# GpSimd's last shift of a D tile written as a 32-bit integer addition

## The chip, the cores and the metric

The program runs on one core of one Trainium2 chip. The metric is the device time of one execution in microseconds (us). A core has five engines that run side by side and wait for each other by semaphores: PE (TensorE, matrix products), ACT (ScalarE), DVE (VectorE), POOL (GpSimd) and SP, which here only issues transfers.

## The reference

```python
def reference(A_x, A_wq, A_wk, A_wv, A_wo, B_x, B_w1, B_b1, B_w2, B_b2):
    def _A_ref(x, wq, wk, wv, wo):          # 2048 rows, 512 columns, 32 heads of 16
        q = (x @ wq).reshape(B, S, H, Dh).transpose(0, 2, 1, 3)
        k = x @ wk                          # one key and one value head for all
        v = x @ wv
        p = softmax(einsum("bhqd,bkd->bhqk", q, k) * (Dh ** -0.5))
        o = einsum("bhqk,bkd->bhqd", p, v)
        return o.transpose(0, 2, 1, 3).reshape(B, S, H * Dh) @ wo
    def _B_ref(x, w1, b1, w2, b2):          # 1792 hidden columns
        return gelu(x @ w1 + b1) @ w2 + b2
    x = A_x
    xn = layernorm(x)
    return x + _A_ref(xn, A_wq, A_wk, A_wv, A_wo) + _B_ref(xn, B_w1, B_b1, B_w2, B_b2)
```

Inputs and output are bf16. All but a small part of the time goes to the exponentials of the scores: 32 heads by 2048 by 2048.

## The kernel before

The prologue loads x in 16 tiles of 128 rows, normalizes them, transposes them on PE into `xnT`, and makes the keys `KT` (L829, ACT copies them out of PSUM), the values `V` and the first queries `QT`. Then comes the main loop. A score tile is 128 keys by 512 queries of one head; there are 2048 of them, taken in 683 units of three. For each unit PE makes the scores (L958) in one of two sets of three PSUM banks, so the scores of unit u+2 need every tile of unit u to have left its bank. A table in the source says which tiles go to which engine:

- ACT takes most of them: one exponential over two or three tiles (L981), written to `E`.
- DVE takes the others in another way. L1012 adds a constant to the scores and writes them as int16 to `Dt`; the bits of such a number, read as bf16, are a first approximation to the exponential (a "pattern"). Four more patterns come from it by adding small whole numbers to the 16-bit words. Two instructions on DVE make three of them in other buffers (L1059, over a batch of tiles); the last one, minus 26, is made in place, one instruction for each tile of 128x512 (L1055). Each pattern is multiplied with its own scaled copy of the values on PE (L1025), and the sum is the better approximation. The shift in place must wait until PE has read the unshifted pattern and DVE has made the others from it.

Between the units, PE also does the queries of later blocks, the two dense layers and the output projection (L672 and others), and DVE brings their results out of PSUM (L1071, L1139, L1167). L1102 on POOL normalizes the attention's output. L1336 are products with zeros that fill stretches in which PE would stand idle.

The order on every engine is fixed when the program is built. A planner (`Prog.schedule`) walks over all operations with costs of its own, and the engines then run that order. Three of its rules matter here. A shift in place (kind "pl") is put on POOL only beside a DVE instruction that is planned for 0.4 us or more and isn't itself a shift; the planned cost is `PL_OCC` = 0.62 us. If a shift has stood ready for 1.0 us, DVE takes it over (L1055 as DVE, planned at 0.2 us). And an operation of the prologue with a due time goes by that time only among those that are ready at the same moment: a free engine takes what there is. The prologue's operations on POOL are added by `setup`, and the due times of the rest (`DU`, `HP`, `QK`, `YP`) are numbers in the source. `add` records an operation with what it reads and writes, and the waits follow from that.

Of the kernel before, what the change touches and what calls it, by code (L numbers as in the profile page):

```python
# [7 lines left out]
ALU = mybir.AluOpType  # L8
AX = mybir.AxisListType

P = 128
# [7 lines left out]
SPL_STEPS = ((1, 0, 1, 26), (2, 0, 2, 51), (0, 0, 1, -26))  # L19
# [16 lines left out]
PL_OCC = 0.62  # L36
ON_OCC = 0.66
PL_LAT = 0.06
# [3 lines left out]
PL_DUE = 3.0  # L42
# [57 lines left out]
TBW = 512  # L100


def vcost(n, mode=1):
    return n / 0.96e3 / mode + 0.065
# [7 lines left out]
class Prog:  # L112
# [19 lines left out]
    def add(self, eng, fn, r=(), w=(), acc=None, dma=None, occ=0.1, lat=0.15, allow=1.0, kind=None, tag=None, after=(), due=None, lock=False, docc=0.0):  # L132
        op = _Op()
        op.lock, op.docc = lock, docc
        op.eng, op.fn = eng, fn
        op.stream = dma or eng
        op.amt = 16 if dma else 1
        op.need = bool(dma)
        op.ticket = None
        op.occ, op.lat, op.allow, op.kind, op.tag = occ, lat, allow, kind, tag  # L140
        op.idx = len(self.ops)
        op.done = False
        op.due = due
        op.rel = None
        op.pm = any(k == ("bank", 7) or k[0] == ("bank", 7) for k in w)
        deps, sdeps = {}, {}

        def dep(o, raw):
            if o is None or o is op:
                return  # L150
            if o.stream == eng == "pe":
                sdeps.setdefault(id(o), (o, False))
                return
            deps[id(o)] = o
            sdeps[id(o)] = (o, True)

        for k in r:
            dep(self.writer.get(k), True)
            for o in self.accs.get(k, ()):
                dep(o, True)  # L160
        for k in w:
            dep(self.writer.get(k), False)
            for o in self.readers.get(k, ()):
                dep(o, False)
            for o in self.accs.get(k, ()):
                dep(o, False)
        if acc is not None:
            dep(self.writer.get(acc), False)
            for o in self.readers.get(acc, ()):
                dep(o, False)  # L170
        op.deps = list(deps.values())
        for o in op.deps:
            o.need = True
        for k in w:
            self.writer[k] = op
            self.readers[k] = []
            self.accs[k] = []
        for k in r:
            self.readers.setdefault(k, []).append(op)
        if acc is not None:  # L180
            self.accs.setdefault(acc, []).append(op)
        for o in after:
            sdeps.setdefault(id(o), (o, True))
        if self.in_chain:
            o = self.chain.get(eng)
            if o is not None:
                sdeps.setdefault(id(o), (o, False))
            self.chain[eng] = op
        op.sdeps = list(sdeps.values())
        self.ops.append(op)  # L190
        return op
# [344 lines left out]
def bass_parallel_sum__grouped_kv_mqa__dense_activation_gelu__prompt_kernel(  # L536
# [15 lines left out]
    S, D = xf.shape  # L552
# [15 lines left out]
    i16, i32 = dt.int16, dt.int32  # L568

    with ExitStack() as es:  # L570
        def sb(shape, dtype, name):
            return es.enter_context(nc.sbuf_tensor(name, shape, dtype))
# [55 lines left out]
        mT = sb([32, TBW], bf, "mT")  # L628
        E = sb([P, NE, TBW], bf, "E")
        Dt = sb([P, ND + (SPL_NB - 1) * NR, TBW], i16, "Dt")  # L630
        Of = sb([P, 2, TBW], f32, "Of")
        den = sb([P, 2, 2, 16], f32, "den")
        OfP = sb([P, 2, TBW], f32, "OfP")
# [13 lines left out]
        add = pr.add  # L647

        def B(b):
            return ("bank", b)  # L650
# [32 lines left out]
        for i in range(8):  # L683
            e = X_Q[i]
            dma("sp" if e == "s" else "act", x_sb[:, 2 * i:2 * i + 2, :], x_view[:, 2 * i:2 * i + 2, :], f"d_x{i}",
                w=[("x", 2 * i), ("x", 2 * i + 1)], lat=X_LAT[i], due=0.0)
# [6 lines left out]
        def setup(fn, r=(), w=(), occ=0.16, due=0.0, lat=0.1, **kw):  # L693
            return add("pool", fn, r, w, occ=occ, lat=lat, due=due, **kw)
# [3 lines left out]
                                        pattern=[[-1, P]], channel_multiplier=1), r=["ident"], w=["ident"])  # L698
        setup(lambda e: e.memset(ones[:], 1.0), w=["ones"])
        zop = setup(lambda e: e.memset(zeros[:], 0.0), w=["zeros"])  # L700
        setup(lambda e: e.memset(mask4[:], 1.0), w=["mask4"])
        setup(lambda e: e.affine_select(out=mask4[:], in_=mask4[:], compare_op=ALU.is_ge, fill=0.0, base=0,
                                        pattern=[[-32, 4]], channel_multiplier=1), r=["mask4"], w=["mask4"])
# [8 lines left out]
              w=[(k, g, j) for k in ("QT", "QTm") for g in range(NGR) for j in range(HG)])  # L712
# [170 lines left out]
        for _, _, kind, a in sorted(steps, key=lambda s: s[:2]):  # L883
# [15 lines left out]
            due=0.0)  # L899
# [6 lines left out]
        for va, vb_ in ((0, NVA), (NVA, NT)):  # L906
            src = vsrc(va, vb_)
            dve(lambda e, src=src, va=va, vb_=vb_: e.tensor_copy(Vf[:, va:vb_, :], src), w=[vbank(va, vb_)[1], ("Vf", va)], n=(vb_ - va) * Dh,
                due=DU["vf"])
# [26 lines left out]
        def tile_of(t):  # L936
            gg, r = divmod(t, TPG)
            return gg, r // HG, r % HG
# [60 lines left out]
        dptr, size, base = [0, 0], [0], [0, 0]  # L999
# [24 lines left out]
        def pv_mm(gg, j, v, kt, rhs, r):  # L1024
# [2 lines left out]
                r=r + [("V", v, 0 if kt < NVA else NVA)], acc="O", occ=0.216, lat=dlat[1],  # L1027
                allow=4.0 if gg < NTB * NGR - 1 or kt < NT - 4 else -5.0, kind="pv", tag=(gg, j))

        def close_batch():  # L1030
            n = len(batch)
            have = {0: 0}

            def slot(b):
                return base[0] if b == 0 else ND + (b - 1) * NR + base[1]

            def view(b, nb):
                s = slot(b)
                step = (slot(b + 1) - s if nb > 1 else n) * TBW
                return bass.AP(Dt[:].tensor, Dt[:].offset + s * TBW, [list(Dt[:].ap[0]), [step, nb], [1, n * TBW]])  # L1040

            def sums(bufs):
                for b in bufs:
                    v = 1 + SPL_K.index(have[b])
                    for q, (t, _) in enumerate(batch):
                        gg, kt, j = tile_of(t)
                        pv_mm(gg, j, v, kt, Dt[:, slot(b) + q, :].bitcast(bf), [(("D", base[b > 0] + q), b)])

            for o, i, nb, k in SPL_STEPS:
                def keys(b):  # L1050
                    return [(("D", base[b + m > 0] + q), b + m) for m in range(nb) for q in range(n)]
                if o == i:
                    for q in range(n):
                        d = Dt[:, slot(o) + q, :]
                        add("pool", lambda e, d=d, k=k: e.tensor_scalar(d, d, 1.0, float(k), ALU.mult, ALU.add),  # L1055
                            [], [(("D", base[o > 0] + q), o)], occ=PL_OCC, lat=PL_LAT, allow=PL_DUE, kind="pl", lock=True,
                            docc=vcost(TBW, 4))
                else:
                    dve(lambda e, d=view(o, nb), q=view(i, nb), k=k: e.tensor_scalar(d, q, float(k), None, ALU.add),  # L1059
                        r=keys(i), w=keys(o), n=nb * n * TBW, mode=4, allow=1.0, kind="post", lock=True)  # L1060
                for m in range(nb):
                    have[o + m] = have[i + m] + k
                sums(range(o, o + nb))
            del batch[:]
# [257 lines left out]
        for i in (0, 1, 3, 2):  # L1322
            dst, key = ub[:, 6 + i, :], ("u", 0, 6 + i)
            w = [(B(FB[i]), j) for j in range(4)] + ([B(FB[i])] if i < 3 else []) + [key]
# [50 lines left out]
```

## Time and profile before

| | |
|---|---|
| time, median of 3 runs | 747.64 us (747.59 to 747.67) |
| the profiled execution's own time | 747.55 us |
| its span, first to last instruction | 745.8 us |
| busy on PE, DVE, ACT | 98% each |
| busy on POOL | 52% |
| shifts in place on POOL (L1055) | 459, 350.7 us busy |
| shifts in place on DVE (L1055) | 98, 25.7 us busy |
| granted TensorE clock | 1.0 all through |

A row of the groups reads: line, engine, operation, what is written and read, shapes, count, then busy time and the mean of one instruction, then the idle time of that engine just before them and who ended it. A row of the timeline begins with the start and the duration in us. Instructions of one engine overlap a little in these records: a DVE instruction that lasts 0.68 us is followed 0.60 us after its start by the next one. So the price of an instruction on a full engine is the distance from its start to the next start.

### The profile page before, as it was taken

The page shows a single profiled execution, that of the slowest core. Times are in us where ns is not written, and L with a number is a line of the kernel's source. Part 1 is how long each engine was busy: PE and PEld are TensorE (multiplying, and loading weights), DVE is VectorE, ACT ScalarE, POOL GpSimd, SP SyncE. Part 2 cuts the span into 40 slices and gives each one's busy share as a digit, 9 for nine tenths or more (in the row PEclk, how much of TensorE's full clock was granted, in tenths as well). Part 3 has the DMA queues.
Part 4 walks back from the last instruction along what each step waited for, and adds up shares of the span by engine and source line. Part 5 has one row for each costly group of instructions (what it writes and reads, how often), then busy time and mean ns, then how long its engine had stood idle before and what let it go on. Part 6 is the DMA issues. An engine that isn't in the chain of part 4 may idle for free.

```text
span 745.8 us, 22104 instructions
## 1 busy us (share of the span) xinstructions
PE 731.8 (98%) x9048; PEld 218.3 (29%) x9050; DVE 732.7 (98%) x1432; ACT 730.9 (98%) x743; POOL 391.4 (52%) x543
## 2 busy tenths in 40 slices
PE   7999999999999999999999999999999999999998
PEld 5322222222232222222232222322333222222223
DVE  8899999999999999999999999999999999999997
ACT  8899999999999999999999999999999999999995
POOL 5455555656433556555555455465564545646541
PEclk9999999999999999999999999999999999999999
DMA  9200100100010010100101010100100101010011
GB/s 312 66 9 24 32 8 18 24 10 16 16 46 22 18 39 17 25 16 16 27 10 28 25 38 17 37 18 12 23 16 19 34 18 38 16 40 23 11 31 36
DMA packets 32078, 23.34 MB, mean 31 GB/s; under 512 B 16369, under 2 KB 27498, under 8 KB 31978
## 3 DMA queue, kind: packets, MB, share of 16 engines
q1 hardware_dynamic: 30922, 21.90, 11.2%
q8 instruction: 72, 1.18, 0.7%
q14 instruction: 28, 0.23, 0.1%
q10 hardware_dynamic: 1056, 0.03, 0.1%
HBM read 13.08 MB, written 2.35 MB: 21 GB/s over the span
## 4 chain that ended last, share of the span: by engine, by line
ACT 61%; PE 30%; DVE 7%; issue 0%; DMA 0%; SPq 0%; POOL 0%
ACT E L981 60%; PE pAll L1025 13%; PE pAll L958 9%; PE pAll L672 7%; DVE Dt L1012 3%; DVE Dt L1059 2%; DMA x_sb<-in_A_x_dram 0%; DVE x_sb L1167 0%; ACT x_sb L1179 0%; PE pAll L810 0%; DVE stats L759 0%; ACT xnT L815 0%; PE pAll L666 0%; DVE Dt L1055 0%; DVE Of L1071 0%
## 5 line engine op out<-in xcount | busy, mean ns | idle before, releaser
L981 ACT ACTIVATE E<-pAll 128x1024 bf16<-128x1024 f32 (+1 forms) x677 | 680.0, 1263 | 1.9 <-PE pAll L958 1.8
L1055 POOL TENSOR_SCALAR Dt<-Dt 128x512 int16<-128x512 int16 x459 | 350.7, 764 | 303.1 <-DVE Dt L1059 128.4
L1025 PE MATMUL pAll<-Dt,V 128*32 128x512 bf16 x2785 | 406.2, 383 | 0.9 <-DVE Of L1071 0.5
L1012 DVE TENSOR_SCALAR Dt<-pAll 128x512 int16<-128x512 f32 (+1 forms) x545 | 368.6, 691 | 2.1 <-PE pAll L958 1.0
L1025 PE MATMUL pAll<-E,V 128*32 128x512 bf16 x1491 | 293.1, 383 | 0.0
L1059 DVE TENSOR_SCALAR Dt<-Dt 128x1024 int16<-128x1024 int16 (+5 forms) x560 | 292.3, 548 | 0.2
L958 PE MATMUL pAll<-QT,KT 32*128 32x512 bf16 x2048 | 267.1, 384 | 4.1 <-ACT E L981 0.9
L958 PEld LDWEIGHTS pAll<-QT,KT 32*128 32x128 bf16 x2048 | 66.7, 91 | 293.9 <-ACT E L981 283.1
L1025 PEld LDWEIGHTS pAll<-Dt,V 128*32 128x32 bf16 x2785 | 102.0, 95 | 101.5 <-issue 68.2
L672 PE MATMUL pAll<-xnT,w_sb 128*32 128x512 bf16 x896 | 85.0, 383 | 0.1
L1025 PEld LDWEIGHTS pAll<-E,V 128*32 128x32 bf16 x1491 | 69.4, 94 | 44.3 <-issue 32.2
L672 PE MATMUL pAll<-w_sb,x_sb 128*32 128x512 bf16 x448 | 68.0, 383 | 0.0
L672 PE MATMUL pAll<-w_sb,ub 128*32 128x512 bf16 x448 | 67.1, 383 | 0.2 <-DVE x_sb L1213 0.2
L672 PE MATMUL pAll<-wop,oTp 128*32 128x512 bf16 x256 | 56.8, 383 | 0.0
L1102 POOL TENSOR_TENSOR oTp<-OfP,rbP 128x256 bf16<-128x256 f32 x29 | 24.1, 837 | 27.2 <-DVE Dt L1055 14.6
L672 PEld LDWEIGHTS pAll<-xnT,w_sb 128*32 128x32 bf16 x896 | 22.1, 95 | 27.0 <-issue 16.3
L1055 DVE TENSOR_SCALAR Dt<-Dt 128x512 int16<-128x512 int16 x98 | 25.7, 281 | 0.0
L672 PE MATMUL pAll<-xnT,wq_sb 128*32 128x512 bf16 x256 | 23.2, 384 | 0.2 <-DVE ub L1167 0.2
L1071 DVE COPY Of<-pAll 128x512 f32<-128x512 f32 x31 | 21.1, 679 | 0.0
L1167 DVE TENSOR_SCALAR x_sb<-pAll,b1T 128x512 bf16<-128x512 f32 x28 | 20.7, 741 | 0.0
L1167 DVE TENSOR_SCALAR ub<-pAll,b1T 128x512 bf16<-128x512 f32 x28 | 20.7, 738 | 0.1
L672 PEld LDWEIGHTS pAll<-w_sb,x_sb 128*32 128x32 bf16 x448 | 16.8, 95 | 10.3 <-issue 7.9
(121 smaller groups left out, 261.9 us busy)
## 6 DMA issues: line engine op xcount, KB each, us to landing
OfP<-Of SPq DMA_DIRECT2D x124, 32.0 KB, 2.0
rbP<-rden_rows SPq DMA_DIRECT2D x124, 32.0 KB, 1.8
w_sb<-in_B_w_dram SPq DMA_DIRECT2D x2, 1792.0 KB, 12.8
x_sb<-in_A_x_dram SPq DMA_DIRECT2D x8, 256.0 KB, 4.3
x_sb<-in_A_x_dram SPq DMA_DIRECT2D x16, 128.0 KB, 2.2
QT<-qp SPq DMA_DIRECT2D x124, 16.0 KB, 1.8
out_dram<-x_sb SPq DMA_DIRECT2D x12, 128.0 KB, 1.9
wq_sb<-in_A_wq_dram SPq DMA_DIRECT2D x1, 512.0 KB, 6.2
```

The source lines that it names most:

```text
L672: add("pe", lambda e, c=c, j=j: e.matmul(o[c, :], l[:, c], rh, start=start, stop=stop, tile_position=(0, 32 * j)), r, [(k, j) for k in w] ...
L958: ins = e.matmul(o, l, rh, start=True, stop=True, tile_position=(q0, 0))
L981: o = act(lambda e: e.activation(E[:, s0:s0 + na, :], bank(b0, na).rearrange("p (a n) -> p a n", a=na), ACT.Exp, scale=LN2 / 128.0), w=[B( ...
L1012: op = dve(lambda e: e.tensor_scalar(Dt[:, s:s + n, :], bank(bk, n).rearrange("p (a n) -> p a n", a=n), float(127 * 128) + SPL_D, SPL_MIN, ...
L1025: add("pe", lambda e, a, b: e.matmul(pO[32 * j:32 * j + 32, :], V1[:, v, kt, :], rhs, start=a, stop=b, tile_position=(0, 32 * j)), r=r + [ ...
L1055: add("pool", lambda e, d=d, k=k: e.tensor_scalar(d, d, 1.0, float(k), ALU.mult, ALU.add), [], [(("D", base[o > 0] + q), o)], occ=PL_OCC, ...
L1059: dve(lambda e, d=view(o, nb), q=view(i, nb), k=k: e.tensor_scalar(d, q, float(k), None, ALU.add), r=keys(i), w=keys(o), n=nb * n * TBW, m ...
L1071: dve(lambda e: e.tensor_copy(Of[:, i, :], pO), w=["O", ("Of", i)], allow=0.0)
L1102: "pool", lambda e, c=c: e.tensor_tensor(oTp[0:n, sl, c], OfP[0:n, s, c], rbP[0:n, s, c], ALU.mult),
L1167: dve(lambda e: e.tensor_scalar(ubs[tb % 2][:, ft, :], pM, b1T[:, ft:ft + 1], None, ALU.add), r=["b1T"], w=M4 + [ukey(tb, ft)], n=TBW + 57 ...
```

## The change

The shift in place stays what it is for the values: minus 26 on each 16-bit pattern. On POOL it is now one integer addition on 32-bit words, each of which holds two patterns, so 256 words for a tile instead of 512 numbers. The second operand is one word, `k32`, read again and again (step 0). Its low half is -26 and its high half -27: the patterns are never under 64, so the low half always carries one into the high half, which makes -26 there too. `k32` is set by two more instructions on POOL. Where DVE takes a shift over, it runs the same instruction as before. The planned costs, the batches and the table of tiles are as they were.

```diff
+        k32 = sb([P, 2], i16, "k32")
...
         zop = setup(lambda e: e.memset(zeros[:], 0.0), w=["zeros"])
+        setup(lambda e: e.memset(k32[:, 0:1], SPL_STEPS[-1][3]), w=["k32"], due=24.0)
+        setup(lambda e: e.memset(k32[:, 1:2], SPL_STEPS[-1][3] - 1), w=["k32"], due=24.0)
         setup(lambda e: e.memset(mask4[:], 1.0), w=["mask4"])
...
+        def last_shift(e, d, k):
+            if e is not nc.gpsimd:
+                return e.tensor_scalar(d, d, 1.0, float(k), ALU.mult, ALU.add)
+            w = k32[:].bitcast(i32)
+            w = bass.AP(w.tensor, w.offset, [list(w.ap[0]), [0, TBW // 2]])
+            return e.tensor_tensor(d.bitcast(i32), d.bitcast(i32), w, ALU.add)
...
                         d = Dt[:, slot(o) + q, :]
-                        add("pool", lambda e, d=d, k=k: e.tensor_scalar(d, d, 1.0, float(k), ALU.mult, ALU.add),
-                            [], [(("D", base[o > 0] + q), o)], occ=PL_OCC, lat=PL_LAT, allow=PL_DUE, kind="pl", lock=True,
+                        add("pool", lambda e, d=d, k=k: last_shift(e, d, k),
+                            ["k32"], [(("D", base[o > 0] + q), o)], occ=PL_OCC, lat=PL_LAT, allow=PL_DUE, kind="pl", lock=True,
                             docc=vcost(TBW, 4))
```

The two new instructions also move others, since the planner takes a new course from the point where they stand. In the changed kernel the lines have other numbers: L702 and L703 set `k32`, the shift in place is L1038 on POOL and L1035 on DVE, L1012 is now L1015, L1059 is L1069, L829 is L832, L981 is L984.

On POOL in the prologue, about where the masks are made, the order was:

```order
L724 MEMSET crow 1x128
L728 MEMSET sel8 128x128
L729 MEMSET mask8 128x8
L725 MEMSET V1 128x96x16
L762 TENSOR_SCALAR nm<-sm 128x1
L730 AFFINE_SELECT mask8<-mask8 128x8
L727 MEMSET V1 128x16
L732 AFFINE_SELECT mask8<-mask8 128x8
```

It is now:

```order
L727 MEMSET crow 1x128
L731 MEMSET sel8 128x128
L732 MEMSET mask8 128x8
L702 MEMSET k32 128x1
L733 AFFINE_SELECT mask8<-mask8 128x8
L703 MEMSET k32 128x1
L735 AFFINE_SELECT mask8<-mask8 128x8
L728 MEMSET V1 128x96x16
L765 TENSOR_SCALAR nm<-sm 128x1
```

The two settings of `k32` have a due time of 24, yet stand where the masks are made, since POOL has a free moment there; the long setting of `V1` goes behind them.

On ACT at the prologue's end, where the keys (`KT`) are copied and the first exponentials (`E`) start, the order was:

```order
L815 ACTIVATE xnT<-pAll 128x4x256 x2
L829 ACTIVATE KT<-pAll,krow 128x512
L840 ACTIVATE oTp<-pAll 128x224
L844 ACTIVATE oTp,kmax<-pAll 128x16 x2
L829 ACTIVATE KT<-pAll,krow 128x512
L829 ACTIVATE KT<-pAll,krow 128x256
L981 ACTIVATE E<-pAll 128x1024
L829 ACTIVATE KT<-pAll,krow 128x512
L981 ACTIVATE E<-pAll 128x1024 x6
```

It is now:

```order
L818 ACTIVATE xnT<-pAll 128x4x256 x2
L843 ACTIVATE oTp<-pAll 128x224
L847 ACTIVATE oTp,kmax<-pAll 128x16 x2
L832 ACTIVATE KT<-pAll,krow 128x512 x2
L984 ACTIVATE E<-pAll 128x1024 x4
L832 ACTIVATE KT<-pAll,krow 128x256
L984 ACTIVATE E<-pAll 128x1536
L832 ACTIVATE KT<-pAll,krow 128x512
L984 ACTIVATE E<-pAll 128x1024 x6
```

One copy of keys moves from ahead of the squares (L840, now L843) to behind them, and one from ahead of the first exponential to behind the fourth.

The third place is the start of the main loop, POOL first. The order was:

```order
L921 TENSOR_SCALAR sel8R<-sel8,R2 128x128
L924 MEMSET wol 128x512
L925 CAST selL<-ident 128x4
L1055 TENSOR_SCALAR Dt<-Dt 128x512
L929 MEMSET b2row 128x512
L1055 TENSOR_SCALAR Dt<-Dt 128x512 x45
```

It is now:

```order
L924 TENSOR_SCALAR sel8R<-sel8,R2 128x128
L927 MEMSET wol 128x512
L928 CAST selL<-ident 128x4
L932 MEMSET b2row 128x512
L1038 TENSOR_TENSOR Dt<-Dt,k32 128x256 x33
```

And DVE in the same stretch, where it now has:

```order
L1069 TENSOR_SCALAR Dt<-Dt 128x512 x2
L1069 TENSOR_SCALAR Dt<-Dt 128x2x512 x2
L1015 TENSOR_SCALAR Dt<-pAll 128x512
L1035 TENSOR_SCALAR Dt<-Dt 128x512 x5
L1015 TENSOR_SCALAR Dt<-pAll 128x512
L1177 TENSOR_SCALAR ub<-pAll,b1T 128x512
```

Before POOL's first instruction on `oTp` there were 46 shifts in place on POOL, and there are 33. The thirteen others are on DVE: 111 of them in the whole program, where there were 98. All thirteen stand among the first 84 instructions of L1012. From there to the end the order is that of before on every engine: of DVE's instructions the last 1222 are the same in the same order, of PE's the last 7809, of ACT's the last 664. Up to there PE has 60 products with zeros of L1336 where it had 12, and in the prologue 29 of L1334 where it had 22; the other operations are the same ones, in another order.

## The prediction

> **What bounds the kernel now.** I read the page first, then the busy time by stretches, then the groups, then single rows of the timeline.
>
> ```profile
> PE 731.8 (98%) x9048; PEld 218.3 (29%) x9050; DVE 732.7 (98%) x1432; ACT 730.9 (98%) x743; POOL 391.4 (52%) x543
> ACT 61%; PE 30%; DVE 7%; issue 0%; DMA 0%; SPq 0%; POOL 0%
> core 0: us, PE busy (x) PEld busy (x) DVE busy (x) ACT busy (x) POOL busy (x), PEclk, DMA share, GB/s
> 30.00:106.00 76.00, 75.27 (x907) 21.82 (x909) 75.80 (x146) 76.00 (x75) 39.52 (x54) 1.00 0.08 20
> 106.00:725.00 619.00, 614.90 (x7678) 176.40 (x7670) 617.51 (x1183) 617.31 (x599) 329.72 (x427) 1.00 0.10 23
> L981 ACT ACTIVATE E<-pAll 128x1024 bf16<-128x1024 f32 x540 | 526.4, 1178 | 1.9 <-PE pAll L958 1.8
> L1055 POOL TENSOR_SCALAR Dt<-Dt 128x512 int16<-128x512 int16 x459 | 350.7, 764 | 303.1 <-DVE Dt L1059 128.4 <-PE pAll L1025 61.3 <-DVE Dt L1012 39.8
> L1012 DVE TENSOR_SCALAR Dt<-pAll 128x512 int16<-128x512 f32 x539 | 358.5, 679 | 2.1 <-PE pAll L958 1.0
> ```
>
> The chain ends on ACT for 61% of the span and on DVE for 7%, but that is a choice among equals: from 106 to 725 us ACT and DVE both stand idle for less than 2 us of 619. Each unit's scores wait for both, so a delay on either is paid nearly whole. POOL is idle for 303 us ahead of its shifts. Making POOL's instruction shorter therefore gains nothing by itself; what counts is what a POOL shift does to DVE.
>
> What it does shows where a POOL shift is still running when DVE begins a shift of its own (L1059). Three such meetings, each the shift on DVE and the POOL shift, the first one with the L1012 ahead of it:
>
> ```profile
> 93.23 0.68 DVE L1012 TENSOR_SCALAR Dt<-pAll 128x512 int16<-128x512 f32 x1
> 93.83 0.41 DVE L1059 TENSOR_SCALAR Dt<-Dt 128x1024 int16<-128x1024 int16 x1
> 93.27 0.62 POOL L1055 TENSOR_SCALAR Dt<-Dt 128x512 int16<-128x512 int16 x1
> ...
> 485.26 0.50 DVE L1059 TENSOR_SCALAR Dt<-Dt 128x1024 int16<-128x1024 int16 x1
> 484.86 0.62 POOL L1055 TENSOR_SCALAR Dt<-Dt 128x512 int16<-128x512 int16 x1
> ...
> 615.87 0.65 DVE L1059 TENSOR_SCALAR Dt<-Dt 128x1024 int16<-128x1024 int16 x1
> 615.61 0.62 POOL L1055 TENSOR_SCALAR Dt<-Dt 128x512 int16<-128x512 int16 x1 [2.50 <-PE pAll L1025]
> ```
>
> POOL ends 0.06, 0.22 and 0.36 us after DVE's shift has begun, and that shift lasts 0.41, 0.50 and 0.65: nothing, 0.09 and 0.24 us too long. So an overlap is free up to 0.13 us, and beyond that DVE waits for POOL's end. The planner lays each POOL shift (0.62) into one L1012 (0.60 from start to start), as in the first meeting. There is hardly any room behind it.
>
> **The change part by part.** Part A is the POOL instruction itself. No row shows a 32-bit integer addition; these are the nearest:
>
> ```profile
> L1055 POOL TENSOR_SCALAR Dt<-Dt x459: 620/622/2059, 28.0 to 732.8; 128x512 int16<-128x512 int16 x153
> L1102 POOL TENSOR_TENSOR oTp<-OfP,rbP x29: 719/783/1374, 94.4 to 718.5; 128x256 bf16<-128x256 f32 x29
> L782 POOL TENSOR_TENSOR nmr<-nm,rstd x4: 192/278/367, 5.4 to 16.6; 128x1 f32<-128x1 f32 x3, 128x2 f32<-128x2 f32 x1
> L875 POOL COPY oTp<-wq_sb 128x256 bf16<-128x256 bf16 x1 | 0.4, 393 | 0.0
> L914 POOL TENSOR_SCALAR V<-oTp 128x256 bf16<-128x256 f32 x5 | 4.3, 865 | 5.5 <-DVE oTp L908 5.1
> ```
>
> Now: 512 numbers, one input, 0.62 undisturbed. New: 256 words, two inputs of 4 bytes, the second one a repeated word. L1102 has that form (256 numbers, two inputs of 4 bytes): its shortest took 0.719, and 14 of its 29 lie between that and 0.740. Against the 0.192 of one number (L782) this is (0.719 - 0.192) / 255 = 2.07 ns a number, where the shift in place takes (0.620 - 0.192) / 511 = 0.84 ns. Half as many elements at 2.5 times the price is no gain. I take 0.727, the middle of those fourteen: 0.107 longer than now. The bounds are 0.393 (256 numbers with one input, L875) and 0.865 (256 numbers in pieces of 16, L914).
>
> The Trainium skill says the same against the change ("GPSIMD Engine Reference", section 3.1): a two-input instruction on GpSimd costs about 2.6 cycles an element, because both operands come through one read port. As an estimate from that page, 256 x 2.6 / 1.2 GHz is 0.55 us, and 0.19 for the start makes 0.75; the sum would then be 755.0 instead of 753.7.
>
> What a longer shift costs I counted on the trace. For each of the 459 POOL shifts I took its end and the start of the next shift on DVE; what a lengthening pushes beyond the free 0.13 us is paid. Today 20 of them are over, for 1.7 us. At +0.06 it is 1.4 us more, at +0.107 54 are over and it is 3.6 us more, at +0.15 6.2, at +0.20 14.0 (208 over), at +0.245 23.7. It is a cliff, since the slots were laid out for 0.62. At 0.393 almost all of today's 1.7 us goes: -1.6. Forecast for A: +3.6. Nothing of it is hidden, by the stretches above.
>
> PE waits for POOL's result only rarely:
>
> ```profile
> PEld pAll L958 <- ACT E L981: 283.1, 658, 0.9
> PEld pAll L1025 <- POOL Dt L1055: 2.7, 12, 0.2
> ```
>
> Twelve waits of at most 0.2 would become longer by 0.1, some 1.3 us in all, and that hides in the 283 us that PE waits for ACT's banks; if that cover were gone, 1.3 us is the price. Taken at nothing.
>
> Part B is the thirteen shifts that go from POOL to DVE at the start of the main loop. Such a shift is followed after 0.20 us:
>
> ```profile
> 315.25 0.28 DVE L1055 TENSOR_SCALAR Dt<-Dt 128x512 int16<-128x512 int16 x1
> 315.45 0.42 DVE L1059 TENSOR_SCALAR Dt<-Dt 128x1024 int16<-128x1024 int16 x1
> 24.40 0.69 DVE L1012 TENSOR_SCALAR Dt<-pAll 128x512 int16<-128x512 f32 x1 [0.43 <-PE pAll L958]
> 27.00 0.69 DVE L1012 TENSOR_SCALAR Dt<-pAll 128x512 int16<-128x512 f32 x1 [0.35 <-PE pAll L958]
> ```
>
> 13 x 0.20 = 2.6 us. Hidden would be what falls into DVE's two waits at the start, 0.43 + 0.35 = 0.8; from 30 to 106 us it is busy for 75.80 of 76.00 and hides nothing. The twelve additional groups of four products with zeros on PE (48) cost 0.21 each if PE had no gap for them, 2.5 in all:
>
> ```profile
> 301.32 0.40 PE L1336 MATMUL pAll<-xnT,zeros 128*32 128x512 bf16 x4
> 302.24 0.61 PE L1336 MATMUL pAll<-xnT,zeros 128*32 128x512 bf16 x8
> ```
>
> They lie in PE's wait for ACT, and I take nothing for them. Bounds for B: 1.8 to 5.1; taken 2.6, since most of the thirteen stand in the full stretch.
>
> Part C is the prologue. Two settings of 0.10 us stand ahead of the long one of `V1` on POOL, whose users come later; POOL has 0.5 us free right behind:
>
> ```profile
> L715 POOL MEMSET epsc<- 128x1 f32 x1 | 0.1, 102 | 0.0
> 8.74 0.30 POOL L777 TENSOR_SCALAR nm<-mv 128x2 f32<-128x2 f32 x1 [0.51 <-DVE mv L773]
> 20.10 0.58 ACT KT L829
> 21.85 0.69 ACT L829 ACTIVATE KT<-pAll,krow 128x512 bf16<-128x512 f32 x1 [0.45 <-PE pAll L666]
> 23.38 0.47 ACT L829 ACTIVATE KT<-pAll,krow 128x256 bf16<-128x256 f32 x1 [0.84 <-PE pAll L666]
> 24.39 1.02 ACT L981 ACTIVATE E<-pAll 128x1024 bf16<-128x1024 f32 x1 [0.54 <-PE pAll L958]
> ```
>
> The wait for `k32` is over long before the first shift at 28 us. The new order is another matter. It takes the copy of keys at 20.10 off the chain that ends last (0.58 gained), and it puts the smaller copy behind four exponentials (0.47 more on a full ACT). I set these against each other: 0, between -0.6 and +0.5.
>
> Sum: the profiled execution took 747.55 (span 745.8), 0.09 below the median of 747.64. 747.55 + 3.6 + 2.6 + 0 = 753.75, say 753.7. By the same bounds, A of 1.4 to 7.2 (+0.06 to +0.16) and B with C of 1.2 to 4, the forecast's own range is 750.2 to 758.7.
>
> **The rivals.** *The addition is quick.* If integers go through like a copy, 0.393 for 256 words, DVE never waits: 747.55 - 1.6 + 2.6 = 748.5. For it speaks that whole words need no conversion; against it that the second input must be read too, and L1102 pays for that. The Trainium skill ("GPSIMD Engine Reference", section 4.1) calls such an addition native, and section 3.1 has short loops at about one cycle an element; no row of this case shows it.
>
> *The addition is slow.* From about +0.16 the slots of the planner no longer hold. At 0.865 as in L914: 747.55 + 23.7 + 2.6 = 773.9. For it speaks that the integer path may be less polished than the usual one; against it that L914 reads and writes in short pieces, which this one doesn't.
>
> *The new start is quicker, and the kernel faster.* Between 21 and 25 us ACT waits for 0.45 + 0.84 + 0.54 = 1.8 us. In the new order both large copies of keys stand there in a row. If ACT sets the pace in the first units, those 1.8 us are work brought forward and the thirteen shifts run beside it. With a quick addition: 747.55 - 1.8 - 1.6 = 744.2; with A as forecast 749.4. It decides for faster when the addition takes less than about 0.63. Against it: behind 30 us DVE is as full as ACT.
>
> **How the numbers follow.** Forecast 0.55, quick addition 0.17, slow 0.18, quicker start 0.10. 0.2% is 1.5 us, about what a measurement of this kernel can tell from no change. Slower: the forecast (0.55), the slow case (0.18), and a quarter of the quick one with B above its middle (0.04): 0.77. Within: most of the quick one (0.11) and part of the last (0.04): 0.15. Faster: 0.06 + 0.02 = 0.08. The range: 748 leaves out the faster part and some of the quick case (about 0.1), 765 the upper half of the slow case (0.09).
>
> **What would show it.** Right: POOL's shifts 446, shortest between 0.71 and 0.75; L1059 on DVE with a larger mean in the same shapes, by some 4 us in sum from 106 us on, with the same orders there; DVE's L1055 111 times; from 0 to 106 us some 2.6 us more. Wrong: a shortest POOL shift near 0.4 (then the gain is at most 1.6) or above 0.8 (then the cliff); a first exponential well before 24.4 us; a DVE that waits for PE by the amount that the collisions cost, so that it was ACT's pace all along.

## The result, and the profile after

| | before | changed |
|---|---|---|
| time, median | 747.62 us (747.58 to 747.67, 4 runs) | 753.62 us (753.60 to 753.70, 4 runs) |
| span of the profiled execution | 745.8 us | 751.9 us |

The ratio is 1.0080 (95% interval 1.0068 to 1.0093): 6.0 us slower, and within 0.1 us of the forecast. The runs below show that this agreement is an accident: the forecast's largest term is zero, and what cost the time isn't in its sum.

The page of the changed kernel, busy times and four groups (L961 makes the scores, as L958 did before; a row reads line, engine, operation, written and read, count, then busy us and mean ns, then idle time ahead of them and who ended it):

```profile
PE 736.3 (98%) x9105; PEld 218.4 (29%) x9105; DVE 735.7 (98%) x1445; ACT 732.0 (97%) x743; POOL 371.7 (49%) x532
L984 ACT ACTIVATE E<-pAll 128x1024 bf16<-128x1024 f32 (+1 forms) x677 | 681.2, 1255 | 5.5 <-PE pAll L961 5.2
L1038 POOL TENSOR_TENSOR Dt<-Dt,k 128x256 int32<-128x256 int32 x446 | 331.3, 755 | 326.7 <-DVE Dt L1069 149.4
L1015 DVE TENSOR_SCALAR Dt<-pAll 128x512 int16<-128x512 f32 (+1 forms) x545 | 370.2, 694 | 4.8 <-PE pAll L961 3.3
L1069 DVE TENSOR_SCALAR Dt<-Dt 128x1024 int16<-128x1024 int16 (+5 forms) x560 | 292.3, 549 | 0.2
```

The durations of the integer addition (shortest, median, longest in ns), from the view of one line:

```profile
L1038 POOL TENSOR_TENSOR Dt<-Dt,k x446: 605/613/2051, 43.4 to 738.9; 128x256 int32<-128x256 int32 x149
```

Two stretches of the changed kernel, the same two as the prediction shows of before:

```profile
30.00:106.00 76.00, 74.97 (x893) 21.79 (x891) 73.05 (x148) 73.23 (x73) 25.54 (x37) 1.00 0.09 20
106.00:725.00 619.00, 614.87 (x7685) 175.44 (x7682) 617.46 (x1183) 617.31 (x600) 322.65 (x431) 1.00 0.10 23
```

Three things are to be seen. The addition takes 0.605 us at its shortest and 0.613 at the median, a little *less* than the old shift (0.620 and 0.622). L1069, DVE's own shifts, add up to 292.3 us, and it was 292.3 before: they are not longer by 4 us. And from 106 us on DVE and ACT are as busy as before (617.51 and 617.31 there). What is new lies ahead of 106 us: ACT is idle for 76.00 - 73.23 = 2.8 us of a stretch where it had no gap, and L984 waits 5.2 us for PE in the whole program where L981 waited 1.8.

The start of an exponential, compared with the start of the one with the same number in the kernel before, tells where the delay grows. The first is 0.32 us late, the third 0.75, the seventh 3.28, the thirteenth 4.21, the twenty-first 5.11, the thirty-third (64 us) 6.11; the hundredth is 6.07 late, and so is the last. So 0.32 us come from the prologue (in six later runs with the prologue of before the first exponential starts between 0.20 earlier and 0.04 later) and 5.75 from the first forty units of the loop.

The wait view of ACT between 24 and 106 us says for whom (total us, times, longest):

```profile
ACT E L984 <- PE pAll L961: 3.9, 8, 0.6
```

And the timeline of ACT shows when. First the start, in single rows:

```profile
24.71 1.02 ACT L984 ACTIVATE E<-pAll 128x1024 bf16<-128x1024 f32 x1
26.23 1.02 ACT L984 ACTIVATE E<-pAll 128x1024 bf16<-128x1024 f32 x1 [0.49 <-PE pAll L961]
27.74 1.02 ACT L984 ACTIVATE E<-pAll 128x1024 bf16<-128x1024 f32 x1 [0.49 <-PE pAll L961]
29.26 1.02 ACT L984 ACTIVATE E<-pAll 128x1024 bf16<-128x1024 f32 x1 [0.49 <-PE pAll L961]
30.18 0.47 ACT L832 ACTIVATE KT<-pAll,krow 128x256 bf16<-128x256 f32 x1
30.88 1.45 ACT L984 ACTIVATE E<-pAll 128x1536 bf16<-128x1536 f32 x1 [0.23 <-PE pAll L961]
32.38 0.69 ACT L832 ACTIVATE KT<-pAll,krow 128x512 bf16<-128x512 f32 x1
```

PE's score products in the same stretch, and the loads of weights (PEld) that stand in front of them:

```profile
25.79 0.39 PE L961 MATMUL pAll<-QT,KT 32*128 32x512 bf16 x3 [0.54 <-DVE Dt L1069]
27.31 0.39 PE L961 MATMUL pAll<-QT,KT 32*128 32x512 bf16 x3
25.79 0.10 PEld L961 LDWEIGHTS pAll<-QT,KT 32*128 32x128 bf16 x3 [0.81 <-ACT E L984]
27.30 0.10 PEld L961 LDWEIGHTS pAll<-QT,KT 32*128 32x128 bf16 x3 [0.43 <-ACT E L984]
```

And the remaining four of ACT's eight waits, from its grouped timeline:

```profile
39.20 1.45 ACT L984 ACTIVATE E<-pAll 128x1536 bf16<-128x1536 f32 x1 [0.60 <-PE pAll L961]
41.25 7.55 ACT L984 ACTIVATE E<-pAll 128x1024 bf16<-128x1024 f32 x7 [0.60 <-PE pAll L961]
49.34 11.66 ACT L984 ACTIVATE E<-pAll 128x1024 bf16<-128x1024 f32 x11 [0.54 <-PE pAll L961]
61.50 9.41 ACT L984 ACTIVATE E<-pAll 128x1024 bf16<-128x1024 f32 x9 [0.49 <-PE pAll L961]
```

ACT and PE take turns here. An exponential starts at 24.71 and ends at 25.73. PE begins the next scores at 25.79, when it is over, and the next exponential starts 0.44 us after that, at 26.23. (The first row of the products puts PE's idle time down to a shift on DVE; the loads of weights for the same products name ACT's exponential.) One turn takes 1.52 us, where two such exponentials in a row take 0.92 (shown with the ninth run). That is what happens when two units in a row use the same set of banks: PE has no second set to fill while ACT empties the first.

The planned order of the exponentials, by units (even units use one set, odd units the other), with the pairs that follow each other on one set:

```
before:  0 2 1 4 3 6 5 8 7 10 9 12 11 14 13 16 15 ...
changed: 0 2 4 6 8 10 1 12 3 14 5 7 9 16 11 18 13 20 15 17 22 19 24 21 26 23 28 25 30 27 29 32 31 ...
pairs, before:  0-2
pairs, changed: 0-2 2-4 4-6 6-8 8-10   5-7 7-9   15-17   27-29
```

The nine pairs of the changed order are the nine places in question: 26.23, 27.74, 29.26, 30.88, 32.97 (there a copy of keys fills the gap), 39.20, 41.25, 49.34 and 61.50. Why six even units come first can be read from the source: the keys' products go through bank 4, which belongs to the odd set, so no odd unit can start ahead of the last of them, and its copy now stands behind the fifth exponential. The odd units then had to catch up, and each one that caught up made another pair. The pair 0-2 stands in both orders; before, a copy of keys lies between its exponentials. So eight pairs are new.

The size fits as well, roughly. The eight steps with a wait (from one exponential's start to the next one's) are 5.0 us longer than such a step without one, the steps right behind them 0.8 in sum, and one more copy of keys stands behind the first exponential (30.18, 0.4 us on a full ACT). Less the 0.3 us by which the order of before falls short of an even pace, that is 5.9, against 5.75 measured.

### The profile page after: what moved, and what is told of

Its sections match the earlier page's. It is cut to its first block, busy times and chain, and to the rows that moved or that the text cites. A ratio compares the mean times of both kernels' runs of the same rounds, so it can differ in the third digit from the quotient of the medians.

```text
span 751.9 us, 22222 instructions
## 1 busy us (share of the span) xinstructions
PE 736.3 (98%) x9105; PEld 218.4 (29%) x9105; DVE 735.7 (98%) x1445; ACT 732.0 (97%) x743; POOL 371.7 (49%) x532
## 4 chain that ended last, share of the span: by engine, by line
ACT 60%; PE 29%; DVE 10%; issue 1%; DMA 0%; SPq 0%
ACT E L984 58%; PE pAll L1028 12%; PE pAll L961 9%; PE pAll L673 6%; DVE Dt L1015 4%; DVE Dt L1069 3%; PE pAll L1346 1%; DMA x_sb<-in_A_x_dram 0%; PE pAll L667 0%; DVE Dt L1035 0%; DVE x_sb L1177 0%; ACT x_sb L1189 0%; DVE stats L762 0%; ACT xnT L818 0%; DVE ub L1177 0%
## 5 line engine op out<-in xcount | busy, mean ns | idle before, releaser
L984 ACT ACTIVATE E<-pAll 128x1024 bf16<-128x1024 f32 (+1 forms) x677 | 681.2, 1255 | 5.5 <-PE pAll L961 5.2
L1038 POOL TENSOR_TENSOR Dt<-Dt,k 128x256 int32<-128x256 int32 x446 | 331.3, 755 | 326.7 <-DVE Dt L1069 149.4
L1015 DVE TENSOR_SCALAR Dt<-pAll 128x512 int16<-128x512 f32 (+1 forms) x545 | 370.2, 694 | 4.8 <-PE pAll L961 3.3
L1069 DVE TENSOR_SCALAR Dt<-Dt 128x1024 int16<-128x1024 int16 (+5 forms) x560 | 292.3, 549 | 0.2
L961 PE MATMUL pAll<-QT,KT 32*128 32x512 bf16 x2048 | 267.1, 384 | 4.5 <-ACT E L984 0.7
L961 PEld LDWEIGHTS pAll<-QT,KT 32*128 32x128 bf16 x2048 | 66.6, 90 | 294.8 <-ACT E L984 282.9
L673 PE MATMUL pAll<-xnT,w_sb 128*32 128x512 bf16 x896 | 84.0, 383 | 0.4 <-DVE ub L1177 0.2
L673 PE MATMUL pAll<-w_sb,x_sb 128*32 128x512 bf16 x448 | 68.0, 383 | 0.0
L673 PE MATMUL pAll<-w_sb,ub 128*32 128x512 bf16 x448 | 67.1, 383 | 0.2 <-DVE x_sb L1223 0.2
L673 PE MATMUL pAll<-wop,oTp 128*32 128x512 bf16 x256 | 56.8, 383 | 0.0
L673 PEld LDWEIGHTS pAll<-xnT,w_sb 128*32 128x32 bf16 x896 | 21.7, 95 | 28.0 <-issue 16.5
L1035 DVE TENSOR_SCALAR Dt<-Dt 128x512 int16<-128x512 int16 x111 | 28.9, 283 | 0.0
L673 PE MATMUL pAll<-xnT,wq_sb 128*32 128x512 bf16 x256 | 24.0, 384 | 0.0
L673 PEld LDWEIGHTS pAll<-w_sb,x_sb 128*32 128x32 bf16 x448 | 16.8, 95 | 10.3 <-issue 7.9
```

What stands on the lines that cost most here:

```text
L673: add("pe", lambda e, c=c, j=j: e.matmul(o[c, :], l[:, c], rh, start=start, stop=stop, tile_position=(0, 32 * j)), r, [(k, j) for k in w] ...
L961: ins = e.matmul(o, l, rh, start=True, stop=True, tile_position=(q0, 0))
L984: o = act(lambda e: e.activation(E[:, s0:s0 + na, :], bank(b0, na).rearrange("p (a n) -> p a n", a=na), ACT.Exp, scale=LN2 / 128.0), w=[B( ...
L1015: op = dve(lambda e: e.tensor_scalar(Dt[:, s:s + n, :], bank(bk, n).rearrange("p (a n) -> p a n", a=n), float(127 * 128) + SPL_D, SPL_MIN, ...
L1035: return e.tensor_scalar(d, d, 1.0, float(k), ALU.mult, ALU.add)
L1038: return e.tensor_tensor(d.bitcast(i32), d.bitcast(i32), w, ALU.add)
```

## The experiments

The theories at the start: the *longer instruction* (part A of the prediction), the *thirteen shifts* on DVE (part B), and a third, that the *order* costs by something else. Each time was taken in five rounds beside the kernel before, on the same chip.

**One: the integer addition in the order of before.** The two settings of `k32` are put into the operation that sets `epsc`, so that the planner has the same operations as before and makes the same order.

```diff
-        setup(lambda e: e.memset(k32[:, 0:1], SPL_STEPS[-1][3]), w=["k32"], due=24.0)
-        setup(lambda e: e.memset(k32[:, 1:2], SPL_STEPS[-1][3] - 1), w=["k32"], due=24.0)
...
-        setup(lambda e: e.memset(epsc[:], 1e-5), w=["epsc"], due=2.0)
+        def set_k32_epsc(e):
+            e.memset(k32[:, 0:1], SPL_STEPS[-1][3])
+            e.memset(k32[:, 1:2], SPL_STEPS[-1][3] - 1)
+            return e.memset(epsc[:], 1e-5)
+
+        setup(set_k32_epsc, w=["epsc", "k32"], due=2.0)
```

> The integer addition on POOL in the order of before: k32 is set together with epsc, as one step of the planner, so that PE, DVE, ACT and SP run exactly the order of before. The recorded sum (a POOL shift 0.107 longer) expects 751.2. The theory that the whole loss lies in the order expects 747.6, within 0.3, since the shortest POOL shift is 0.605 in the trace of the change against 0.620 before.

Measured: 747.45 us, ratio 0.9999 (0.9991 to 1.0008). The addition, by the view of its line:

```profile
L1041 POOL TENSOR_TENSOR Dt<-Dt,k x459: 603/612/2052, 27.8 to 732.7; 128x256 int32<-128x256 int32 x153
```

All 459 additions are there, and the time is that of before. Part A is zero.

**Two: the old shift in the new order.**

```diff
-            if e is not nc.gpsimd:
+            if True:
                 return e.tensor_scalar(d, d, 1.0, float(k), ALU.mult, ALU.add)
```

> The changed kernel's order on every engine, k32 set but not used: the shifts on POOL are the tensor_scalar instruction of before. The recorded sum expects 750.1 (only the thirteen shifts on DVE). The theory of the order expects 753.6, within 0.3.

Measured: 753.69 us, ratio 1.0081 (1.0068 to 1.0095). The whole loss is in the order, whatever instruction POOL runs.

**Three: `k32` set late.** The two settings wait until the prologue's other settings on POOL are through.

```diff
-        setup(lambda e: e.memset(k32[:, 0:1], SPL_STEPS[-1][3]), w=["k32"], due=24.0)
-        setup(lambda e: e.memset(k32[:, 1:2], SPL_STEPS[-1][3] - 1), w=["k32"], due=24.0)
...
+        setup(lambda e: e.memset(k32[:, 0:1], SPL_STEPS[-1][3]), w=["k32"], due=24.0, after=late)
+        setup(lambda e: e.memset(k32[:, 1:2], SPL_STEPS[-1][3] - 1), w=["k32"], due=24.0, after=late)
```

> The change with k32 held back until the first query mask is there (like wol and b2row), so that the planner gives PE, DVE, ACT and SP the order of before and only two short settings more stand on POOL. The recorded sum expects 751.2, the theory of the order 747.6, within 0.4.

Measured: 747.5 us, ratio 0.9999 (0.9990 to 1.0008). Two instructions of 0.1 us cost 6 us in one place of the plan and nothing in another.

**Four: the changed order, its fourteen early shifts back on POOL.** (Fourteen went to DVE and one came back; the fourteen are meant.)

```diff
         pr.schedule()
+        shifts = sorted((o for o in pr.ops if o.kind != "fill" and o.docc), key=lambda o: o.idx)
+        for n in (0, 2, 3, 4, 5, 6, 12, 16, 18, 19, 20, 23, 29, 42):
+            assert shifts[n].eng == "dve"
+            shifts[n].eng = shifts[n].stream = "pool"
```

> The changed kernel's order, but the fourteen early shifts that went from POOL to DVE are back on POOL, at the same place of the sequence. If thirteen shifts on DVE cost 0.20 each, 751.0 (2.6 less than 753.6). If the units in the wrong order set the time of this stretch alone and DVE has room there, 753.6. If these shifts stand behind POOL's later ones and are waited for, more than 753.6.

Measured: 755.32 us, ratio 1.0104 (1.0089 to 1.0120), 1.7 us more than the changed kernel. In this order the shifts are better off on DVE, so they can't be what costs 2.6 us there. Three of ACT's waits behind 45 us, by its timeline:

```profile
48.04 1.45 ACT L984 ACTIVATE E<-pAll 128x1536 bf16<-128x1536 f32 x1 [0.33 <-PE pAll L961]
50.21 11.60 ACT L984 ACTIVATE E<-pAll 128x1024 bf16<-128x1024 f32 x11 [0.72 <-PE pAll L961]
73.10 3.88 ACT L984 ACTIVATE E<-pAll 128x1024 bf16<-128x1024 f32 x3 [0.48 <-PE pAll L961]
```

Two more waits, of 0.33 and of 0.48, and the one that was 0.54 is 0.72. That the shifts come late on POOL and what needs them with them would explain this; it wasn't tried apart.

**Five: the order of before, the same fourteen shifts on DVE.** The edit is that of run four, made in the kernel before, with "dve" and "pool" in each other's place.

> The kernel before, unchanged but for fourteen early shifts in place, which run on DVE at the same place of the order. Theory 'thirteen shifts cost 0.20 us each' (the prediction's part B): DVE is full there, so 14 x 0.20 = 2.8 us, 750.4. Theory 'the order of the first score units costs the 6 us': this order is that of before, so whatever the shifts cost is no part of the 6 us; after the run with the shifts back on POOL (755.3 against 753.6) it expects less than 2.8, 747.6 to 749.

Measured: 749.89 us, ratio 1.0030 (1.0019 to 1.0042). This lies above the 749 that the theory of the order allowed, and close to the 750.4 of the theory of the shifts. The exponentials fall back from 35 us on, by 1.86 us at the forty-first and 2.2 at 106 us. The stretches:

```profile
30.00:106.00 76.00, 74.39 (x877) 21.30 (x879) 75.95 (x155) 74.93 (x74) 30.31 (x40) 1.00 0.09 20
106.00:725.00 619.00, 614.90 (x7684) 176.65 (x7677) 617.55 (x1184) 617.30 (x599) 327.41 (x428) 1.00 0.09 23
```

DVE is busy for 75.95 of 76.00 and ACT has 1.1 us of gaps. So the price of part B was nearly right for the order of before, 2.3 of 2.8 us; it is wrong for the order in which the shifts really stand, where DVE has gaps (73.05 of 76.00 in the changed kernel).

**Six and seven: new prologue with the old loop, old prologue with the new loop.** The planned list of operations is cut at the first score unit (behind 331 operations of before, 334 of the changed kernel) and put together crosswise. Run six sets `k32` as run one does. This is its edit; that of run seven is made in the same way.

```diff
         pr.schedule()
+        START = [14, 24, 0, 1, 9, 2, 16, 15, 25, 17, 47, 3, 18, 21, 19, 22, -1, 20, 4, -1, 23, 28,
...
+        pr.ops = new + pr.ops[331:]
```

> Integer addition on POOL; the prologue in the changed kernel's order up to the first score unit (but with every key copy where it was before), the main loop in the order of before, shifts on the engines of before. Theory 'order of the first score units': only the 0.32 us by which the first exponential starts later remain, 747.9. Theory 'the prologue's new order costs it': nearly all of the 6 us, 753 or more.

> The counterpart: the prologue in the order of before (the keys of tiles 10 and 11 copied ahead of the first exponential), and behind it everything in the changed kernel's order: the last keys' copy behind the sixth exponential, six even units ahead of the first odd one, the shifts on DVE. Theory 'order of the first score units': 753.6 less 0.32 = 753.3. Theory 'the prologue's new order costs it': 748 or less.

Measured: the new prologue with the old loop 749.20 us, ratio 1.0022 (1.0013 to 1.0031); the old prologue with the new loop 754.26 us, ratio 1.0088 (1.0074 to 1.0101). The first one's start on ACT:

```profile
25.52 0.47 ACT L835 ACTIVATE KT<-pAll,krow 128x256 bf16<-128x256 f32 x1 [0.70 <-PE pAll L667]
25.89 1.02 ACT L987 ACTIVATE E<-pAll 128x1024 bf16<-128x1024 f32 x1
27.12 0.69 ACT L835 ACTIVATE KT<-pAll,krow 128x512 bf16<-128x512 f32 x1 [0.21 <-PE pAll L667]
27.71 2.84 ACT L987 ACTIVATE E<-pAll 128x1024 bf16<-128x1024 f32 x3
```

And the second one's:

```profile
25.89 1.02 ACT L984 ACTIVATE E<-pAll 128x1024 bf16<-128x1024 f32 x1 [0.58 <-PE pAll L961]
28.69 1.02 ACT L984 ACTIVATE E<-pAll 128x1024 bf16<-128x1024 f32 x1 [1.78 <-PE pAll L961]
30.21 1.02 ACT L984 ACTIVATE E<-pAll 128x1024 bf16<-128x1024 f32 x1 [0.49 <-PE pAll L961]
31.73 1.45 ACT L984 ACTIVATE E<-pAll 128x1536 bf16<-128x1536 f32 x1 [0.49 <-PE pAll L961]
```

I had expected 747.9 for the first, and it is 1.3 us more: with the smaller copy of keys ahead of it, its first exponential starts at 25.89 (1.50 late). But behind that its loop loses only 0.08 us. The second starts its first exponential 0.11 us *early* and loses 7.0 us in the loop. That is 1.3 more than the 5.75 of the changed kernel, and the row with the wait of 1.78 holds it. In this execution the granted TensorE clock (the third number from the right in a row of the stretches) was 0.50 there:

```profile
25.53:28.95 3.42, 3.42 (x28) 0.84 (x26) 2.00 (x4) 1.28 (x2) 2.68 (x6) 0.50 0.02 5
```

Sixteen products of L673 take PE 1.90 us in that stretch, and 1.05 in the changed kernel, where the clock was 1.00. Of the five runs the one with a mean granted clock of 1.0 took 753.31 us, as the theory of the order had expected (753.3); the four at 0.995 took 754.19 to 754.58. The order of the loop's first units costs the 5.75 us, whichever prologue stands in front.

**Eight: the changed order with the late keys early.** The products and copies of the keys of tiles 10 to 15 go where they were before; the units stay.

```diff
+        early, late = [242, 254, 255, 256, 257, 258], [285, 286, 287, 288, 289]
...
+            if o is at[327]:
+                new += [at[i] for i in early]
+            new.append(o)
+            if o is at[329]:
+                new += [at[i] for i in late]
```

> The changed kernel with only the key products of tiles 10 to 15 and their two copies on ACT put where they were before (ahead of and right behind the first exponential); the units stay in the changed order, six even ones ahead of the first odd one. Theory 'the order of the units on one set of banks': ACT still waits about 0.49 us for PE after each of the even units, 752.5 to 753.8. Theory 'the key copies in between are what ACT and PE wait for': most of the 6 us goes, 748 to 750.

Measured: 755.09 us, ratio 1.0100 (1.0086 to 1.0114), 1.3 us above what the theory of the order allowed. On ACT:

```profile
27.75 1.02 ACT L984 ACTIVATE E<-pAll 128x1024 bf16<-128x1024 f32 x1
29.25 1.02 ACT L984 ACTIVATE E<-pAll 128x1024 bf16<-128x1024 f32 x1 [0.49 <-PE pAll L961]
30.77 1.02 ACT L984 ACTIVATE E<-pAll 128x1024 bf16<-128x1024 f32 x1 [0.49 <-PE pAll L961]
32.29 1.45 ACT L984 ACTIVATE E<-pAll 128x1536 bf16<-128x1536 f32 x1 [0.49 <-PE pAll L961]
```

The keys are there in time, and ACT waits as often, eight times. Its first exponential is 1.54 us late, which makes nearly all of the 1.3 us, and its loop loses 5.9 us, about as much as that of the changed kernel. What costs is the order of the units. That the late keys made the planner choose it is read from its rules and wasn't tried apart.

**Nine: the same fault, made in the full loop.** In the kernel before, eight units between 200 and 406 change places with the one behind them.

```diff
...
+        for a, b in [(200, 201), (229, 230), (257, 258), (294, 295), (321, 322), (346, 347), (371, 372), (405, 406)]:
+            for k in ("S", "E", "p1"):
+                hold[id(found[k, a])] = found[k, b]
...
```

> The kernel before, with eight places in the middle of the main loop (units 200 to 406) where a unit changes places with the one behind it, so that the bank sets run even, even, odd, odd instead of even, odd, even, odd: sixteen pairs of units in a row on one set of banks, all of which have two tiles on ACT and one on DVE. Theory 'two units in a row on one set of banks cost 0.6 us, because PE can make the second one's scores only behind the first one's exponential': 16 x 0.6 = 9.6 us, 757.2, with sixteen waits of about 0.5 us on ACT for PE. Theory 'it was the empty start of the loop (few tiles and batches under way) that cost the time': in the full loop the swaps cost next to nothing, 747.6 to 749.

Measured: 758.28 us, ratio 1.0148 (1.0130 to 1.0166), 10.7 us more; its four runs lie wide apart, from 757.51 to 760.70. One of the eight places on ACT:

```profile
239.01 1.10 ACT L981 ACTIVATE E<-pAll 128x1024 bf16<-128x1024 f32 x1
240.60 1.94 ACT L981 ACTIVATE E<-pAll 128x1024 bf16<-128x1024 f32 x2 [0.49 <-PE pAll L958]
243.04 1.02 ACT L981 ACTIVATE E<-pAll 128x1024 bf16<-128x1024 f32 x1 [0.49 <-PE pAll L958]
```

The two exponentials of the middle row are of different sets: 1.94 us together, so the second starts 0.92 after the first. Ahead of and behind them stands the wait of 0.49, as at the start of the changed kernel. All sixteen pairs have it. Two more waits (0.49 and 0.41) stand at 341.8 and 344.8, right behind one of the places. In this execution the granted TensorE clock was 0.50 there, and 1.00 in the rest of the loop, so they aren't counted as the swaps' price. Whether the swaps bring such a drop on was not tried.

```profile
340.12:343.53 3.41, 3.41 (x28) 0.62 (x28) 2.38 (x6) 2.69 (x3) 0.00 (x0) 0.50 0.02 5
```

The two runs at a mean granted clock of 0.995 and 0.996 took 759.00 (the profiled one) and 760.70 us; the two at 0.998 took 757.51 and 757.57, which is 10.0 us more than before, or 0.63 for each of the sixteen pairs.

The kernel before has two such pairs of its own in the full loop, by its planned order: units 435 and 437, and units 510 and 512. Its trace shows the same wait at both:

```profile
476.79 76.60 ACT L981 ACTIVATE E<-pAll 128x1024 bf16<-128x1024 f32 x76 [0.49 <-PE pAll L958]
553.88 1.02 ACT L981 ACTIVATE E<-pAll 128x1024 bf16<-128x1024 f32 x1 [0.49 <-PE pAll L958]
```

So a pair costs about 0.6 us in the full loop as well, and the empty start isn't needed for it.

**Ten and eleven: what makes the addition short, and what a long one costs.** Run ten adds in the form of L1102 (float32 words, written as bf16), with the repeated word; run eleven adds integers with 256 stored words in place of the repeated one. Both have the order of before.

```diff
-        k32 = sb([P, 2], i16, "k32")
+        k32 = sb([P, 1], f32, "k32")
...
-            w = k32[:].bitcast(i32)
-            w = bass.AP(w.tensor, w.offset, [list(w.ap[0]), [0, TBW // 2]])
-            return e.tensor_tensor(d.bitcast(i32), d.bitcast(i32), w, ALU.add)
+            w = bass.AP(k32[:].tensor, k32[:].offset, [list(k32[:].ap[0]), [0, TBW // 2]])
+            return e.tensor_tensor(d.bitcast(bf)[:, 0:TBW // 2], d.bitcast(f32), w, ALU.add)
```

```diff
-        k32 = sb([P, 2], i16, "k32")
+        k32 = sb([P, TBW], i16, "k32")
...
             w = k32[:].bitcast(i32)
-            w = bass.AP(w.tensor, w.offset, [list(w.ap[0]), [0, TBW // 2]])
```

> The kernel before, with POOL's shift replaced by an addition in the form of the output's normalization: 256 words of 32 bits read as float32, a repeated word added, written as bf16. It leaves out the shift by minus 26 for the tiles on POOL and writes half of each tile. Theory 'a longer POOL instruction pushes DVE's shifts as counted on the trace of before' (the prediction's part A with the row it chose): the shortest takes 0.72 and the time is 3.5 us more, 751.1. Theory 'DVE has slack where they meet': the instruction takes 0.72 and the time stays within 1 us of before. If the shortest is near 0.61, it was not the float words that make the normalization longer.

> The integer addition in the order of before, with a second operand of 256 stored words instead of one word read again and again. Theory 'the repeated word makes the addition quick (0.61 against the 0.72 of the normalization)': the shortest shift is near 0.72 and the time 751. Theory 'integers in, integers out make it quick': 0.61, 747.5.

Measured: float words 747.66 us, ratio 1.0002 (0.9993 to 1.0010); 256 stored words 747.83 us, ratio 1.0004 (0.9995 to 1.0013). The durations, of run ten:

```profile
L1039 POOL TENSOR_TENSOR Dt<-Dt,k x459: 603/614/2053, 27.9 to 732.8; 128x256 bf16<-128x256 f32 x153
```

and of run eleven:

```profile
L1040 POOL TENSOR_TENSOR Dt<-Dt,k x459: 713/732/2167, 27.7 to 733.1; 128x256 int32<-128x256 int32 x153
```

It is the repeated word, not the integers, that makes the addition short. And run eleven has the long addition that the prediction assumed (0.73), yet costs 0.3 us, within the uncertainty, where 3.6 were counted (in its profiled execution the way from the first exponential to the last is 0.48 us longer than before). DVE's shifts in that run:

```profile
L1071 DVE TENSOR_SCALAR Dt<-Dt 128x1024 int16<-128x1024 int16 (+5 forms) x560 | 294.8, 552 | 0.2
```

and its full stretch:

```profile
106.00:725.00 619.00, 614.90 (x7679) 176.66 (x7667) 617.93 (x1183) 617.30 (x599) 367.78 (x427) 1.00 0.09 23
```

The collisions are there: DVE's shifts take 294.8 us where they took 292.3. But DVE is only 0.42 us busier from 106 us on, and ACT not idle for longer (617.30). So DVE had slack for most of it, though it is busy for 98% of the span. Some of the slack can be read from the starts: between 30 and 730 us the distances from one shift on DVE to the next add up to 1.8 us more than in run one, and those from one first pattern (L1012 of before) to the next to 1.15 us less. Where the rest lies wasn't followed.

## Why the prediction was right, and by which wrong steps

**Its number** was right, and its direction too, but by luck. The sum was 3.6 for part A, 2.6 for part B and 0 for part C. The runs show 0 for part A, no cost for part B where its shifts stand, 0.3 for the prologue, and 5.75 for the order of the loop's first units, which is no term of the sum.

**Part A, "I take 0.727 ... 0.107 longer than now"**: failed. The row chosen as nearest, L1102, has two stored operands; the new instruction has one and a repeated word. I named that difference ("the second one a repeated word") and gave it no weight. It is the difference that decides: 0.61 against 0.73 for the same integers.

**"+3.6 ... Nothing of it is hidden"**: failed on its own, for run eleven has that longer instruction. The count of collisions, 3.6 us, wasn't far from how much longer DVE's shifts get, 2.5. The step that failed is the one ahead of it, "a delay on either is paid nearly whole", taken from busy shares of 617 in 619 us. Of these small delays, spread over 600 us, 0.3 to 0.5 us are paid. In run five fourteen shifts of 0.2 us within the first 72 us are paid nearly whole (2.3 of 2.8). That it is the closeness that makes the difference was not tried.

**Part B, thirteen shifts at 0.20 on a full DVE**: mis-sized, and of the other sign in its place. I priced them in the trace of before, where DVE is full from 30 to 106 us; in the changed order it isn't, and with the shifts on POOL the time is 1.7 us more.

**"The twelve additional groups of four products with zeros ... I take nothing for them"**: the price of the products is indeed nothing. But the planner puts them where PE would stand idle, so 48 more of them were the sign that the new order leaves PE without work for longer. I priced the filling and didn't ask for the hole.

**Part C, "between -0.6 and +0.5"**: right for what it covers, the first exponential starts 0.32 us later. It ended one step too early. The order on ACT showed the smaller copy of keys behind four exponentials and the large one behind the fifth. I priced the copies (0.47 more) and didn't ask which units can run while those keys are missing. That step is the missing term of 5.75.

**"B with C of 1.2 to 4"**: the upper end doesn't follow from the prediction's own bounds, which are 5.1 for B and 0.5 for C, 5.6 together. The range would then have ended at 760.3 instead of 758.7.

**The rivals.** The quick addition came true in part: 0.61 us is less than the 0.62 of before, but far from 0.393, and what an addition of 0.393 would gain was not tried. The slow addition is out. The quicker start didn't come; two copies of keys in a row did not shorten ACT's waits, as its timeline of the changed kernel shows:

```profile
22.30 0.69 ACT L832 ACTIVATE KT<-pAll,krow 128x512 bf16<-128x512 f32 x1 [0.82 <-PE pAll L667]
24.12 0.69 ACT L832 ACTIVATE KT<-pAll,krow 128x512 bf16<-128x512 f32 x1 [1.13 <-PE pAll L667]
```

Together 1.95 us, where the three waits of before made 1.83.

**What would show it**: 446 shifts on POOL, 111 on DVE, and the order from there on were right. The shortest shift (0.605 instead of 0.71 to 0.75), the longer L1069 (292.3 both times) and 2.6 us up to 106 us (6.07) were wrong.

No version beat the kernel before: with the order kept, the integer addition is worth nothing (run one), since POOL was no bound.

## What to carry to other kernels

Where a planner reorders the start of a loop with two buffers, list the order of the units by buffer and count the neighbours on the same one: each costs a full hand-over between producer and consumer (0.6 us here), whatever the busy shares say. Two engines that are both busy for 98% hid most of some small delays that were spread over the whole program (run eleven), and paid for work that was added within a few units (run five), so ask where a delay falls before adding it up. A row taken for an instruction that isn't in the trace should have the same operands in memory, not only the same sizes and types.

## What was unexpected of the hardware

GpSimd's two-input operations on 128x256 words of 32 bits, shortest of each kind: integers with a repeated word (run one) 0.603 us, float words to bf16 with a repeated word 0.603, integers with 256 stored words 0.713, float words with 256 stored words (L1102) 0.719. So the type and the conversion make no difference beyond 0.006 us here; reading the second operand from new places costs 0.11 us. Above the 0.192 of a single number, the stored operand makes (0.713 - 0.192) / 255 = 2.04 ns a word and the repeated one 1.61.

The Trainium skill ("GPSIMD Engine Reference", section 3.1) puts a two-input operation at about 2.6 cycles an element; at 1.2 GHz that is an estimate of 2.17 ns. With stored operands this case's runs agree within 6% (2.04 ns); with a repeated word they are a quarter below it.
